# Float64 weights to float32: exponent and low bits made on ScalarE, two merging passes on VectorE

## Chip, cores and metric

The kernel runs on one core of a Trainium2 chip. The metric is the device time of one execution in microseconds; a run's time is that of its core. Engines are named as the profile names them: PE (TensorE matmul), PEld (its weight load), DVE (VectorE), ACT (ScalarE), SP (SyncE, which here issues every transfer).

## What is computed

Attention with 4 sink positions and a window of 128 over 2 batches, 8 heads, 768 positions and head size 64, then two two-layer blocks on the 1536 rows of width 512 that come out of it. The blocks' weights arrive as float64.

```python
x = attention(q, k, v)                  # 1536 x 512
h = x @ w_in                            # 512 x 2048
g = maximum(h, 0) + alpha * minimum(h, 0)
x = g @ w_out                           # 2048 x 512
h = x @ w_in2
out = (h - tanh(h)) @ w_out2
```

## The kernel before

The attention is done in 48 pairs of heads, numbered `n` (a unit of 128 positions has 4 pairs). A pair is scored on PE (`s_mm`), its maximum is taken on DVE (`s_max`), its exponential on ACT (`s_exp`), it is normalised on DVE (`norm`), turned on PE (`t_mm`), copied out of PSUM by ACT (`t_ev`), and multiplied with the values on PE (`pv`). Pairs 0 to 18 run alone (`for n in range(S_LEAD)`, line 526 on); pairs 19 to 47 run inside the blocks.

The blocks are 96 steps `g`: block `m` (0, 1), chunk `c` of 512 rows (3), slice `f` of 128 hidden units (16). Every product is made in three float32r matmuls out of a high and a low part of both factors. Step `g` makes `h` of its slice (`h_mm`, 12 matmuls, line 367) and the output share of the slice of two steps ago (`out_mm`, 12 matmuls, line 419); in steps 0 to 31 it also carries one pair of the attention. For block 0 the result of `h_mm` has one PSUM bank, which ACT empties (`evac_first`, line 374) before the next step's `h_mm` may write it.

Weights: slice `f` of a block is 2 x 512 KB of float64 (`load_w`). It lands in one of two staging halves (`raw`), is converted to float32 (`conv_w`, `convert_weights`, lines 47 to 60) into a `wf` tile that stays for the block's three chunks, and in every step a high part is made on ACT (`split_w`, line 195) and a low part on DVE (`split_lo`, line 200). Each `yield` in `convert_weights` is a place where the conversion may be split: `conv_start` issues the ACT pass, `conv_step` one DVE pass at a time.

```python
    nc.scalar.activation(out=dst, in_=hw.bitcast(F32), func=AF.Abs)          # line 52
    yield
    nc.vector.tensor_scalar(dst, dst, HW_LO, HW_HI, op0=ALU.max, op1=ALU.min)    # line 54
    yield
    nc.vector.tensor_scalar(di, di, 5, 2, ...)                                # line 56
    yield
    nc.vector.scalar_tensor_tensor(di, lw, 29, di, ...)                       # line 58
    yield
    nc.vector.scalar_tensor_tensor(di, hw, TOP2, di, ...)                     # line 60
```

The kernel is scheduled by hand: every engine runs its instructions in the order in which the code issues them. Block 0 is converted during the attention alone (slices 0 and 1, from pairs 8 and 12 on) and in steps 0 to 13 (one slice each); block 1 in steps 31 to 46 (three steps out of four) and three more slices by step 60. In a step of chunk 0 the DVE order is: norm of the pair before, the first conversion pass, `s_max`, `evac_mid`, two `split_lo`, `evac_lo`, the other conversion passes. At the end of the step ACT issues the first pass for the next slice (`conv_start(*ahead)`), and SP the load of the slice after that, which waits until its staging half has been read. In steps 33 and 39 `flag` and `flag_rest` test whether the inputs suit this fast path; the test's result guards a general path that is not taken here.

Of the kernel before, what the change touches and what calls it, by code (L numbers as in the profile page):

```python
# [12 lines left out]
U8 = mybir.dt.uint8  # L13
BF16 = mybir.dt.bfloat16
# [25 lines left out]
TOP2 = -0x40000000  # L40

# [6 lines left out]
def convert_weights(nc, pair, dst):  # L48

    lw, hw = pair[:, :, 0], pair[:, :, 1]  # L50
    di = dst.bitcast(I32)
    nc.scalar.activation(out=dst, in_=hw.bitcast(F32), func=AF.Abs)  # L52
    yield
    nc.vector.tensor_scalar(dst, dst, HW_LO, HW_HI, op0=ALU.max, op1=ALU.min)
    yield
    nc.vector.tensor_scalar(di, di, 5, 2, op0=ALU.logical_shift_left, op1=ALU.logical_shift_right)  # L56
    yield
    nc.vector.scalar_tensor_tensor(di, lw, 29, di, op0=ALU.logical_shift_right, op1=ALU.bitwise_or)  # L58
    yield
    nc.vector.scalar_tensor_tensor(di, hw, TOP2, di, op0=ALU.bitwise_and, op1=ALU.bitwise_or)  # L60

# [59 lines left out]
def fast_path(tc, qk, v, vsink, limits, w1i, w1o, alpha, w2i, w2o, out, outer):  # L121
# [3 lines left out]
    with ExitStack() as ctx:  # L125
# [15 lines left out]
        vs = const.tile([128, 4, 128], F32, name="vs")  # L141
        m_even = const.tile([128, 288], BF16, name="m_even")
# [38 lines left out]
        def conv_w(m, f):  # L181
            raw = stage[m][f % 2]
            if m == 1 and f < 3:
                wf[m, f] = ap.tile([128, 1024], F32, name="wf", tag="wx" if f == 2 else "pq", bufs=1 if f == 2 else 2)
            else:
                wf[m, f] = wp.tile([128, 1024], F32, name="wf", tag="wf", bufs=NF)
            yield from convert_weights(nc, raw.rearrange("p (n t) -> p n t", t=2), wf[m, f])
# [3 lines left out]
        def split_w(m, c, f, part):  # L191
# [3 lines left out]
            nc.scalar.activation(out=hi, in_=src, func=AF.Copy)  # L195
            whl[m, c, f, part] = (hi, lo)

        def split_lo(m, c, f, part):
            hi, lo = whl[m, c, f, part]
            nc.vector.tensor_tensor(lo, wf[m, f][:, 512 * part:512 * part + 512], hi, op=ALU.subtract)  # L200
# [156 lines left out]
        h_ps, gt, o_ps, mid, ob = {}, {}, {}, {}, {}  # L357

        def h_mm(m, c, f, lo, hi):
            x = (x_t, y_t)[m][c]  # L360
            if lo == 0:
                h_ps[f] = ps_tile(["h"] if m == 0 else ["h", "s", "t"])
# [223 lines left out]
        def flag():  # L586
# [8 lines left out]
            nc.vector.tensor_tensor(worst, worst, top, op=ALU.mult)  # L595
            flag_in.extend((ones, worst))
# [3 lines left out]
        def flag_rest():  # L600
            ones, worst = flag_in
            t = ps_tile(["t"])
# [19 lines left out]
        for g in range(N):  # L622
# [25 lines left out]
            if g == 2 * NF + 1:  # L648
                flag()
            if g == 2 * NF + 7:  # L650
# [306 lines left out]
```

## Time and profile before

| | us |
|---|---|
| three runs | 677.49, 677.59, 677.14 (median 677.49) |
| the profiled execution's span | 676.7 |
| its own time | not listed apart; the runs lie 0.4 to 0.9 over its span |
| PE busy in the span | 639.5 (95%) |
| DVE busy | 567.1 (84%) |
| ACT busy | 437.6 (65%) |

The span runs from the first to the last instruction of the program. The shares are means over stretches with different limits, so the stretches are read apart. A matmul of 512 columns is listed with some 0.39 us, though the next one starts 0.23 us after it: matmuls overlap, and the time of a stretch is read from the starts.

### The profile page before, as it was taken

The numbers are of one execution on the slowest core, as the hardware profiler recorded it, in microseconds if no ns is written. First come the engines' busy times: TensorE is split into PE (matmuls) and PEld (weight loads), VectorE is DVE, ScalarE is ACT, GpSimd is POOL, SyncE is SP. The second block draws the span as 40 slices with busy tenths as digits, with TensorE's granted clock in tenths as the row PEclk, the third lists the DMA queues.
The fourth block names the chain that finished last, engine by engine and source line by source line (L and its number), as shares of the span: only waits on it lengthen the run. The fifth ranks groups of instructions, "written<-read, shape, count | busy, mean of one in ns | idle before, by whom it ended". The sixth has DMA issues, their size and how long they took to land.

```text
span 676.7 us, 9202 instructions
## 1 busy us (share of the span) xinstructions
PE 639.5 (95%) x3194; PEld 502.8 (74%) x3194; DVE 567.1 (84%) x1159; ACT 437.6 (65%) x872; POOL 1.1 (0%) x8
## 2 busy tenths in 40 slices
PE   4878999999999999999899999999999999999995
PEld 2556667767777777777687888888888888888884
DVE  5898999999967566648999998999988878888873
ACT  4776766666656565544545557778777777777763
POOL 0000000000000000000000000000000000000000
PEclk9987999999999999999999999999999999999998
DMA  4653343445010000023333340100010000100001
GB/s 110 218 155 96 140 156 140 155 157 186 1 47 17 0 16 1 31 96 112 137 125 125 139 173 0 44 20 0 1 62 1 1 0 1 62 1 1 0 1 67
DMA packets 27031, 47.36 MB, mean 70 GB/s; under 512 B 3168, under 2 KB 15456, under 8 KB 26976
## 3 DMA queue, kind: packets, MB, share of 16 engines
q1 hardware_dynamic: 26976, 46.68, 20.2%
q8 instruction: 27, 0.44, 0.3%
q14 instruction: 28, 0.23, 0.1%
HBM read 43.53 MB, written 3.15 MB: 69 GB/s over the span
## 4 chain that ended last, share of the span: by engine, by line
PE 71%; DVE 18%; DMA 3%; ACT 3%; issue 2%; SPq 2%; ACTq 0%; DVEq 0%
PE ps_o L419 31%; PE ps_h L367 19%; PE ps_s L367 6%; PE ps_t L367 6%; DVE wf L58 3%; DVE wf L60 2%; DMA vt<-in_v_dram 2%; DVE wf L56 2%; DVE gl L403 2%; DVE pq L259 1%; DVE wl L200 1%; PE ps_s L250 1%; PE ps_t L299 1%; DVE pq L283 1%; PE ps_v L338 1%
## 5 line engine op out<-in xcount | busy, mean ns | idle before, releaser
L200 DVE TENSOR_TENSOR wl<-wf,wh 128x512 fp32r<-128x512 f32 x192 | 123.4, 682 | 44.1 <-ACT wh L195 44.1
L367 PE MATMUL ps_h<-x,wh 128*128 128x512 f32 x384 | 124.6, 405 | 4.6 <-ACT t L374 4.1
L195 ACT ACTIVATE wh<-wf 128x512 fp32r<-128x512 f32 x192 | 111.6, 629 | 26.4 <-DVE wf L60 10.1
L367 PEld LDWEIGHTS ps_h<-x,wh 128*128 128x128 f32 x384 | 68.3, 188 | 22.4 <-ACT t L374 7.6
L419 PE MATMUL ps_o<-gh,wh 128*128 128x512 f32 x192 | 76.6, 399 | 1.4 <-DVE y L430 1.4
L367 PE MATMUL ps_h<-x,wl 128*128 128x512 f32 x192 | 75.2, 392 | 0.0
L419 PE MATMUL ps_o<-wh,gh 128*128 128x512 f32 x192 | 74.8, 390 | 0.2 <-ACT gh L398 0.2
L419 PE MATMUL ps_o<-gh,wl 128*128 128x512 f32 x192 | 74.9, 390 | 0.0
L419 PE MATMUL ps_o<-gl,wh 128*128 128x512 f32 x192 | 74.8, 390 | 0.0
L419 PE MATMUL ps_o<-wh,gl 128*128 128x512 f32 x192 | 74.8, 390 | 0.0
L419 PE MATMUL ps_o<-wl,gh 128*128 128x512 f32 x192 | 74.7, 389 | 0.0
L268 ACT ACTIVATE pq<-pq,nm 128x288 f32<-128x288 f32 (+1 forms) x96 | 48.4, 507 | 32.1 <-DVE nm L259 32.1
L398 ACT ACTIVATE gh<-g 128x512 fp32r<-128x512 f32 x48 | 30.4, 633 | 37.7 <-DVE g L109 37.7
L398 ACT ACTIVATE gh<-t 128x512 fp32r<-128x512 f32 x48 | 30.1, 627 | 32.4 <-DVE t L386 32.4
L52 ACT ACTIVATE wf<-raw 128x1024 f32<-128x1024 f32 x32 | 36.7, 1147 | 16.7 <-DMA raw<-in_moe_w_out_dram 16.7
L419 PEld LDWEIGHTS ps_o<-gh,wh 128*128 128x128 f32 x192 | 36.0, 188 | 10.2 <-DVE y L430 1.8
L367 PEld LDWEIGHTS ps_h<-x,wl 128*128 128x128 f32 x192 | 36.0, 188 | 8.2
L419 PEld LDWEIGHTS ps_o<-wh,gh 128*128 128x128 f32 x192 | 36.0, 188 | 8.1 <-ACT gh L398 0.6
L419 PEld LDWEIGHTS ps_o<-wh,gl 128*128 128x128 f32 x192 | 36.0, 188 | 7.9 <-DVE gl L403 0.4
L419 PEld LDWEIGHTS ps_o<-gh,wl 128*128 128x128 f32 x192 | 36.0, 188 | 7.8
L419 PEld LDWEIGHTS ps_o<-wl,gh 128*128 128x128 f32 x192 | 36.1, 188 | 7.4
L419 PEld LDWEIGHTS ps_o<-gl,wh 128*128 128x128 f32 x192 | 36.1, 188 | 7.0
(142 smaller groups left out, 1274.5 us busy)
## 6 DMA issues: line engine op xcount, KB each, us to landing
raw<-in_moe_w_in_dram SPq DMA_DIRECT2D x32, 512.0 KB, 3.3
raw<-in_moe_w_out_dram SPq DMA_DIRECT2D x32, 512.0 KB, 4.3
raw_qk<-in_qk_dram SPq DMA_DIRECT2D x96, 64.0 KB, 3.0
vt<-in_v_dram SPq DMA_DIRECT2D x12, 256.0 KB, 3.1
out_dram<-ob SPq DMA_DIRECT2D x2, 1024.0 KB, 4.3
out_dram<-ob SPq DMA_DIRECT2D x4, 256.0 KB, 3.6
vs<-in_vsink_dram SPq DMA_DIRECT2D x2, 256.0 KB, 3.1
ns_raw<-in_limits_dram SPq DMA_DIRECT2D x1, 2.0 KB, 2.5
```

The source lines that it names most:

```text
L52: nc.scalar.activation(out=dst, in_=hw.bitcast(F32), func=AF.Abs)
L56: nc.vector.tensor_scalar(di, di, 5, 2, op0=ALU.logical_shift_left, op1=ALU.logical_shift_right)
L58: nc.vector.scalar_tensor_tensor(di, lw, 29, di, op0=ALU.logical_shift_right, op1=ALU.bitwise_or)
L60: nc.vector.scalar_tensor_tensor(di, hw, TOP2, di, op0=ALU.bitwise_and, op1=ALU.bitwise_or)
L195: nc.scalar.activation(out=hi, in_=src, func=AF.Copy)
L200: nc.vector.tensor_tensor(lo, wf[m, f][:, 512 * part:512 * part + 512], hi, op=ALU.subtract)
L250: nc.tensor.matmul(sps[n, a][:, :w], lhsT=kq[l][h, p, at:at + 128], rhs=kq[r][h, p, K_EVEN:K_EVEN + w], start=e == 0, stop=e == 2)
L268: nc.scalar.activation(out=e, in_=e, func=AF.Exp, scale=-1.0, bias=nm[:, 2 * n + a:2 * n + a + 1], accum_out=sums[G][:, hh:hh + 1])
L367: nc.tensor.matmul(h_ps[f], lhsT=l[:, w], rhs=x[:, r, kk, :], start=kk == 0 and e == 0, stop=kk == 3 and e == 2)
L398: nc.scalar.activation(out=gh, in_=mid[f], func=AF.Copy)
L403: nc.vector.tensor_tensor(gl, mid.pop(f), gt[f][0], op=ALU.subtract)
L419: nc.tensor.matmul(o, lhsT=l, rhs=r, start=f == 0 and e == 0, stop=f == NF - 1 and e == 2)
```

## The change

For the fast path, `convert_weights` (one ACT pass, four DVE passes) gives way to `convert_scaled` (two ACT passes, two DVE passes). ACT's first pass multiplies the high word, read as a float32, by 2 to the power of -111, which moves the exponent instead of masking it, and sums each row into `seen`; its second pass turns the upper 16 bits of the low word into the number of its top three bits and writes that back over the low word. DVE shifts the first result by 3 and joins the three bits, then joins the sign. The weights are now 256 times too large; `split_w` and `split_lo` take that out by a factor of 1/256, for which `split_lo` becomes a scalar_tensor_tensor. Three small DVE instructions test `seen`, and `flag` and `flag_rest` move from steps 33 and 39 to steps 65 and 71. `flag_rest` uses the PSUM bank `v`, and block 1 takes the banks `h`, `s`, `t` strictly in turn, where before the turn was also advanced by the four output banks of each chunk.

```diff
--- before.py
+++ after.py
@@ -11,6 +11,7 @@
 F32R = mybir.dt.float32r
 I32 = mybir.dt.int32
 U8 = mybir.dt.uint8
+U16 = mybir.dt.uint16
 BF16 = mybir.dt.bfloat16
 AF = mybir.ActivationFunctionType
 ALU = mybir.AluOpType
@@ -38,6 +39,10 @@
 HW_LO = 3.0517578125e-05
 HW_HI = 122879.9921875
 TOP2 = -0x40000000
+SIGN = -0x80000000
+W_UP, W_DOWN = 2.0 ** -111, 2.0 ** -8
+W_LIMIT = 61440.0 * W_UP
+FLOOR = -4095.5 / 8192
 
 P0, P1, P2 = 0.33333329098008546, -0.13331417165962514, 0.052681329087423304
 POLY_T2 = 0.04
@@ -60,6 +65,19 @@
     nc.vector.scalar_tensor_tensor(di, hw, TOP2, di, op0=ALU.bitwise_and, op1=ALU.bitwise_or)
 
 
+def convert_scaled(nc, pair, dst, seen):
+
+    lw, hw = pair[:, :, 0], pair[:, :, 1]
+    top = pair.bitcast(U16)[:, :, 1]
+    di = dst.bitcast(I32)
+    nc.scalar.activation(out=dst, in_=hw.bitcast(F32), func=AF.Abs, scale=W_UP, accum_out=seen)
+    nc.scalar.activation(out=lw, in_=top, func=AF.Copy, scale=1.0 / 8192, bias=FLOOR)
+    yield
+    nc.vector.scalar_tensor_tensor(di, di, 3, lw, op0=ALU.logical_shift_left, op1=ALU.bitwise_or)
+    yield
+    nc.vector.scalar_tensor_tensor(di, hw, SIGN, di, op0=ALU.bitwise_and, op1=ALU.bitwise_or)
+
+
 def load_scalars(nc, pool, limits):
 
     raw = pool.tile([128, 2, 2], I32, name="ns_raw")
@@ -139,6 +157,7 @@
         al = const.tile([128, NF], F32, name="al")
         nm = const.tile([128, 2 * NPAIR], F32, name="nm")
         vs = const.tile([128, 4, 128], F32, name="vs")
+        seen = const.tile([128, 2 * NF], F32, name="seen")
         m_even = const.tile([128, 288], BF16, name="m_even")
         m_odd = const.tile([128, 288], BF16, name="m_odd")
         m_one = const.tile([128, 288], BF16, name="m_one")
@@ -184,7 +203,8 @@
                 wf[m, f] = ap.tile([128, 1024], F32, name="wf", tag="wx" if f == 2 else "pq", bufs=1 if f == 2 else 2)
             else:
                 wf[m, f] = wp.tile([128, 1024], F32, name="wf", tag="wf", bufs=NF)
-            yield from convert_weights(nc, raw.rearrange("p (n t) -> p n t", t=2), wf[m, f])
+            at = m * NF + f
+            yield from convert_scaled(nc, raw.rearrange("p (n t) -> p n t", t=2), wf[m, f], seen[:, at:at + 1])
 
         whl = {}
 
@@ -192,12 +212,12 @@
             src = wf[m, f][:, 512 * part:512 * part + 512]
             hi = wp.tile([128, 512], F32R, name=f"wh{part}", tag=f"wh{part}", bufs=2)
             lo = wp.tile([128, 512], F32R, name=f"wl{part}", tag=f"wl{part}", bufs=2)
-            nc.scalar.activation(out=hi, in_=src, func=AF.Copy)
+            nc.scalar.activation(out=hi, in_=src, func=AF.Copy, scale=W_DOWN)
             whl[m, c, f, part] = (hi, lo)
 
         def split_lo(m, c, f, part):
             hi, lo = whl[m, c, f, part]
-            nc.vector.tensor_tensor(lo, wf[m, f][:, 512 * part:512 * part + 512], hi, op=ALU.subtract)
+            nc.vector.scalar_tensor_tensor(lo, wf[m, f][:, 512 * part:512 * part + 512], W_DOWN, hi, op0=ALU.mult, op1=ALU.subtract)
 
 
         x_t, y_t = {}, {}
@@ -355,11 +375,13 @@
 
 
         h_ps, gt, o_ps, mid, ob = {}, {}, {}, {}, {}
+        turn = [0]
 
         def h_mm(m, c, f, lo, hi):
             x = (x_t, y_t)[m][c]
             if lo == 0:
-                h_ps[f] = ps_tile(["h"] if m == 0 else ["h", "s", "t"])
+                turn[0] += m
+                h_ps[f] = ps_tile(["hst"[turn[0] % 3]])
             wh, wl = whl[m, c, f, 0]
             for kk in range(lo, hi):
                 w = slice(kk * 128, kk * 128 + 128)
@@ -593,13 +615,16 @@
             nc.vector.tensor_scalar(worst, worst, 9e8, None, op0=ALU.is_le)
             nc.vector.tensor_scalar(top, top, 1.0, None, op0=ALU.is_le)
             nc.vector.tensor_tensor(worst, worst, top, op=ALU.mult)
+            nc.vector.tensor_scalar(seen, seen, W_LIMIT, None, op0=ALU.is_lt)
+            nc.vector.tensor_reduce(top, seen, axis=AX.X, op=ALU.min)
+            nc.vector.tensor_tensor(worst, worst, top, op=ALU.mult)
             flag_in.extend((ones, worst))
 
         flag_in = []
 
         def flag_rest():
             ones, worst = flag_in
-            t = ps_tile(["t"])
+            t = ps_tile(["v"])
             nc.tensor.matmul(t[:, 0:1], lhsT=ones, rhs=worst, start=True, stop=True)
             ok = const.tile([1, 2], F32, name="ok")
             lim = const.tile([1, 2], F32, name="lim")
@@ -645,9 +670,9 @@
                 ahead = (1, start.get(g + 1, slow.get(g + 1)))
             if conv1 is not None and conv1 + 2 < NF:
                 load = (1, conv1 + 2)
-            if g == 2 * NF + 1:
+            if g == 4 * NF + 1:
                 flag()
-            if g == 2 * NF + 7:
+            if g == 4 * NF + 7:
                 flag_rest()
 
             if att and n - 2 < NPAIR:
```

VectorE in step 2 of block 0, before (the order of steps 0 to 13 is alike). `sums` and `pq<-pq,sums` are `norm`, ISA is `s_max`, `wl` is `split_lo`, `gl` is `evac_lo`, and `wf` are the conversion passes:

```order
L283 TENSOR_SCALAR pq<-pq,sums 128x288 x2
L54 TENSOR_SCALAR wf<-wf 128x1024
L259 ISA pq,nm<-ps_s,m_odd 128x288
L259 ISA nm 128x1
L259 ISA pq,nm<-ps_t,m_odd 128x288
L259 ISA nm 128x1
L386 SCALAR_TENSOR_TENSOR t<-t,al 128x512
L200 TENSOR_TENSOR wl_934<-wf,wh_933 128x512
L200 TENSOR_TENSOR wl_931<-wf,wh_930 128x512
L403 TENSOR_TENSOR gl<-t,gh 128x512
L56 TENSOR_SCALAR wf<-wf 128x1024
L58 SCALAR_TENSOR_TENSOR wf<-raw_89,wf 128x1024
L60 SCALAR_TENSOR_TENSOR wf<-raw_89,wf 128x1024
```

The same place now:

```order
L303 TENSOR_SCALAR pq<-pq,sums 128x288 x2
L76 SCALAR_TENSOR_TENSOR wf<-wf,raw_90 128x1024
L279 ISA pq,nm<-ps_s,m_odd 128x288
L279 ISA nm 128x1
L279 ISA pq,nm<-ps_t,m_odd 128x288
L279 ISA nm 128x1
L408 SCALAR_TENSOR_TENSOR t<-t,al 128x512
L220 SCALAR_TENSOR_TENSOR wl_932<-wf,wh_931 128x512
L220 SCALAR_TENSOR_TENSOR wl_929<-wf,wh_928 128x512
L425 TENSOR_TENSOR gl<-t,gh 128x512
L78 SCALAR_TENSOR_TENSOR wf<-raw_90,wf 128x1024
```

Of the conversion, one pass stands ahead of `s_max` and one behind `gl`, in place of one and three; `wl` has become a scalar_tensor_tensor.

ScalarE in the same step, before, from `s_exp` (`pq,sums`) to the copy `t_ev` (`pt<-ps_t`) of the next step; `gh` is `evac_hi`, `t<-ps_h` is `evac_first`:

```order
L268 ACTIVATE pq,sums<-pq,nm 128x288 x2
L398 ACTIVATE gh<-t 128x512
L374 ACTIVATE t<-ps_h 128x512
L52 ACTIVATE wf<-raw_89 128x1024
L214 ACTIVATE kq<-raw_qk 128x2x256
L306 ACTIVATE pt<-ps_t 128x512
L195 ACTIVATE wh_1009<-wf 128x512
```

The same place now:

```order
L288 ACTIVATE pq,sums<-pq,nm 128x288 x2
L420 ACTIVATE gh<-t 128x512
L396 ACTIVATE t<-ps_h 128x512
L73 ACTIVATE wf,seen<-raw_90 128x1024
L74 ACTIVATE raw_90<-raw_90 128x1024
L234 ACTIVATE kq<-raw_qk 128x2x256
L326 ACTIVATE pt<-ps_t 128x512
L215 ACTIVATE wh_1006<-wf 128x512
```

The second conversion pass (`raw<-raw`) stands between `evac_first` and what follows it: the next step's `t_ev`, and in every second step a `kq` copy ahead of that.

## Rows read from the trace of the kernel before

**Rows 1.** Stretches between step starts: length, busy PE, PEld, DVE, ACT, POOL; clock, DMA.

```profile
0.00:74.29 74.29, 54.03 (x369) 37.34 (x369) 61.72 (x234) 49.51 (x137) 1.14 (x8) 0.93 0.48 148
74.29:173.66 99.37, 94.12 (x494) 68.79 (x495) 97.64 (x208) 62.58 (x132) 0.00 (x0) 1.00 0.43 147
173.66:189.37 15.71, 15.55 (x88) 11.33 (x86) 12.77 (x31) 8.75 (x21) 0.00 (x0) 1.00 0.00 0
189.37:288.68 99.31, 99.07 (x577) 77.11 (x577) 65.80 (x177) 58.42 (x136) 0.00 (x0) 1.00 0.08 24
302.42:329.69 27.27, 23.79 (x109) 18.47 (x107) 24.10 (x39) 14.22 (x24) 0.00 (x0) 1.00 0.32 116
329.69:363.78 34.09, 33.51 (x147) 27.21 (x147) 32.73 (x53) 19.18 (x30) 0.00 (x0) 1.00 0.34 124
363.78:676.70 312.92, 305.66 (x1345) 251.84 (x1343) 266.09 (x410) 217.72 (x381) 0.00 (x0) 0.99 0.10 35
```

**Rows 2.** Chain that ended last: start us, us, what; two of its pieces.

```profile
346.48 2.72 PE ps_h L367 x12
...
418.34 2.97 PE ps_s L367 x12
```

**Rows 3.** DVE groups by line and shape: busy us, mean ns, idle before.

```profile
L200 DVE TENSOR_TENSOR wl<-wf,wh 128x512 fp32r<-128x512 f32 x192 | 123.4, 682 | 44.1 <-ACT wh L195 44.1
L58 DVE SCALAR_TENSOR_TENSOR wf<-raw,wf 128x1024 int32<-128x1024 int32 x32 | 39.2, 1224 | 0.9
...
L108 DVE SCALAR_TENSOR_TENSOR g<-b,g 128x512 f32<-128x512 f32 x48 | 32.7, 681 | 0.0
...
L54 DVE TENSOR_SCALAR wf<-wf 128x1024 f32<-128x1024 f32 x32 | 22.0, 687 | 1.6 <-ACT wf L52 1.6
```

**Rows 4.** ACT groups by line and shape.

```profile
L52 ACT ACTIVATE wf<-raw 128x1024 f32<-128x1024 f32 x32 | 36.7, 1147 | 16.7 <-DMA raw<-in_moe_w_out_dram 16.7
...
L268 ACT ACTIVATION_READ_ACCUMULATOR pq<-pq,nm 128x1 f32 x96 | 18.1, 189 | 0.0
```

**Rows 5.** DVE in order of time, step 12 and start of step 13 (start us, us).

```profile
161.42 0.17 DVE L274 TENSOR_SCALAR sums<-sums 128x2 f32<-128x2 f32 x1
...
162.38 0.69 DVE L54 TENSOR_SCALAR wf<-wf 128x1024 f32<-128x1024 f32 x1
162.99 0.45 DVE L259 CUSTOM_DVE_ANT_0 pq<-ps_s,m_one 128x288 f32<-128x288 f32 x1
...
169.33 0.16 DVE L274 TENSOR_SCALAR sums<-sums 128x2 f32<-128x2 f32 x1
```

**Rows 6.** ACT in order of time, from step 12 to the `t_ev` of step 13.

```profile
163.48 0.54 ACT L268 ACTIVATE pq<-pq,nm 128x288 f32<-128x288 f32 x1 [1.93 <-DVE nm L259]
...
165.53 1.15 ACT L52 ACTIVATE wf<-raw 128x1024 f32<-128x1024 f32 x1
166.57 0.63 ACT L214 ACTIVATE kq<-raw_qk 128x512 fp32r<-128x512 f32 x1
167.09 0.59 ACT L306 ACTIVATE pt<-ps_t 128x512 f32<-128x512 f32 x1
```

**Rows 7.** PE in step 13: the last score matmul of its pair.

```profile
168.11 0.29 PE L250 MATMUL ps_t<-kq 64*128 64x288 f32 x1
```

**Rows 8.** PE in order of time, 318 to 331 us: the three matmul groups that waited.

```profile
321.11 0.72 PE L367 MATMUL ps_h<-x,wh 128*128 128x512 f32 x2 [0.93 <-ACT t L374]
...
325.49 0.50 PE L419 MATMUL ps_o<-gh,wh 128*128 128x512 f32 x1 [1.35 <-DVE y L430]
...
329.69 0.74 PE L367 MATMUL ps_h<-x,wh 128*128 128x512 f32 x2 [1.21 <-ACT t L374]
```

**Rows 9.** ACT in order of time, the same stretch.

```profile
323.76 2.02 ACT L429 ACTIVATE y<-ps_o 128x512 fp32r<-128x512 f32 x4
```

**Rows 10.** DVE in order of time, the same stretch.

```profile
324.76 2.47 DVE L430 TENSOR_TENSOR y<-ps_o,y 128x512 fp32r<-128x512 f32 x4
...
327.75 0.74 DVE L386 SCALAR_TENSOR_TENSOR t<-t,al 128x512 f32<-128x512 f32 x1
```

## Prediction

> **What bounds the kernel now.** I read the chain that ended last first, then the busy times by stretch, then the groups and the order of time on each engine, to see what a conversion costs and who stands behind it.
>
> The edges of rows 1 are the first matmuls of steps 2, 14, 16, 29, then 31, 35 and 41. In the last half the chain is PE alone: pieces of twelve matmuls of 2.72 us, back to back, two to a step, so 5.44 us a step [rows 2]. No engine that only feeds PE can shorten that. The one blemish is a piece of 2.97, in step 51. The busy times show the same for steps 16 to 28: 99.31 us for 13 steps, 7.64 each with the attention inside, PE busy for 99.07, DVE for 65.80 [rows 1]. These stretches stay as they are.
>
> Steps 2 to 13 are another matter. They take 99.37 us, 8.28 each, and DVE is busy for 97.64 of them, 98% [rows 1]. They are the steps that convert one slice each. Steps 14 and 15, with the same order of code and no conversion, take 15.71 together, 7.86 each. So DVE bounds these twelve steps, by 0.4 us a step over the same code without conversion and by 0.64 over steps 16 to 28. The second such place is steps 31 to 40, where block 1 is converted: DVE is busy for 32.73 of the 34.09 of steps 35 to 40, and just before that three groups on PE waited [rows 1, 8]. What comes ahead of step 2 takes 74.29 us, DVE busy for 61.72, ACT for 49.51: neither engine alone; four slices are converted there.
>
> **The change part by part.** *DVE passes.* A slice loses L54 and L56, two of one form, 2 x 0.687 = 1.37 us [rows 3]. The two merges that remain read one strided and one dense operand, as L58 does, and I give them its 1.224. `split_lo` (L200) turns from 0.682 [rows 3] into a scalar_tensor_tensor with constants; that form on the same size takes 0.681 (L108), so nothing.
>
> *ACT passes.* The first pass stays (1.147 [rows 4]) and gains a row sum; the sum's read-out is the accumulator row, 0.189. The second pass is new. Its read is strided like that of L52, of which 1024 elements take 1.147; its write goes to every second word, and no row shows ACT writing so. From below 1.04, what L52 holds ACT up to the next start, 165.53 to 166.57 [rows 6]; from above 2.3, twice L52, if the strided write cost as much again as the read. I take 1.15, since strided reads and dense writes of the same count are the nearest row. The Trainium skill, page "SBUF — State Buffer", section "Door 1: The DMA port swizzle", says that accesses that fall at least twice into one 16-byte line go at full rate; words 8 bytes apart do, so by it the second pass would cost an estimated 1.15 and the sum below would stand, while a write that missed that rate would make it about 674. No row tells the two apart.
>
> So a slice gives DVE 1.37 back and gives ACT 0.19 + 1.15 = 1.34. What matters is who stands behind ACT. Behind the second pass wait, on ACT, the `kq` copy and `t_ev` of the next step; behind `t_ev` waits PE's next `s_mm` (its bank is the one that `t_ev` empties), behind that `s_max` on DVE, behind that `s_exp`, again on ACT. That ring closes once a step. Its present length: `s_exp` starts at 163.48, `t_ev` at 167.09 and ends at 167.68 [rows 6], the last score matmul ends at 168.40 [rows 7], and `s_max` to `s_exp` takes 0.49 (162.99 [rows 5] to 163.48), so the next `s_exp` could start at 168.89: 5.41 us, against the 7.91 that DVE needs from one `norm` to the next (161.42 to 169.33 [rows 5]). With 1.34 more the ring is 6.75, and 7.3 in the one step of four that has an `x` copy there. It stays under PE's 7.64. The first merge on DVE also waits for the second pass, but `norm` stands ahead of it and covers it: 0.96 from 161.42 to 162.38.
>
> *Steps 2 to 13.* DVE's need falls from 97.64 by 12 x 1.37 to 81.2, 6.8 a step. PE is then the longest. The gain is at least nothing and at most what PE's own work leaves: six of the twelve steps have the short first units of the second batch in them, with about 0.5 less attention than the 7.64 of steps 16 to 28, so 7.4 on average and 12 x (8.28 - 7.4) = 10.5. I choose 7.78 a step, just under the 7.86 of the steps without conversion, since rings this close to each other (6.8, 6.75 to 7.3, 7.4) don't run without loss: 12 x 0.5 = 6.0. Steps 14 and 15 start without a backlog on DVE: 0.3.
>
> *Ahead of step 2.* Four slices at 1.37 are 5.5 on DVE and 5.4 more on ACT. In the attention alone neither engine is full, and an ACT pass is on the way of `t_ev` and `s_exp` at once, while the DVE passes that go were spread over several pairs. From -2 to 4; I take 1.5, most of it in steps 0 and 1, which have the DVE order of the steps above.
>
> *Steps 31 to 40.* The three waits of PE end at 321.11, 325.49 and 329.69 and are 0.93 + 1.35 + 1.21 = 3.5 [rows 8]; steps 35 to 40 lose another 34.09 - 6 x 5.44 = 1.45 in small ones [rows 1]. All of it is DVE's backlog. I follow what replaces it. The conversion ahead of the copies of `y` holds ACT some 2.35 us instead of 1.1, but is reached 2.2 earlier, since the two merges before it end earlier; so the four copies, now at 323.76 [rows 9], start at about 322.9. DVE's part of them, 324.76 to 327.2 [rows 10], then ends at about 325.9, the first merge (1.24, where L54 took 0.6) at 327.2, and `evac_mid` starts there instead of at 327.75. So of the first three waits only 0.55 is won; the later ones, 1.45, go, as a step then needs 5.1 on DVE. Together 2.0, between 0 and 4.95. Step 51 loses its late bank: 2.97 - 2.72 = 0.25 [rows 2].
>
> *The flag.* Some ten small DVE instructions go from step 33 to step 65 and three come along. DVE is busy for 266.09 of the last 312.92 [rows 1], so they are covered; uncovered they would cost some 0.17 each, like the small DVE row at 161.42 [rows 5], 2.2 us.
>
> Sum: 6.0 + 0.3 + 1.5 + 2.0 + 0.25 = 10.05. The profiled span is 676.7; the median of the runs lies 0.8 over it, at 677.5. 676.7 - 10.0 + 0.8 = 667.5 us.
>
> **The rivals.** *The second pass is dear, and ACT's ring takes over (slower).* The ring without it is 5.41 + 0.19 = 5.6; it passes the present 8.28 once the pass costs over 2.7 us, 2.3 times L52. At 3.4 (three accesses for one) it is 9.0: 12 x 0.7 = 8.6 lost, some 4 ahead of step 2, so 690. For it speaks only that no row shows such a write; against it that the strided read costs hardly more than a dense one. Chance 0.06.
>
> *An exchange without profit.* 1.37 of DVE is paid with 1.34 of ACT; if ACT's passes hold up the pairs as much as DVE's did, or the pass costs 2.3 (ring 7.9, 8.4 with `x`), the time stays between 675 and 679. Against it: ACT is busy for 62.58 of 99.37 in steps 2 to 13 [rows 1]. Beside it stands the Trainium skill, page "ScalarE: Activation LUTs", section "Rules for kernel authors", which wants `max`, `min`, `add` and `mul` on VectorE and not on ScalarE. By that rule the time would stay at about 677; the rows agree on the price of one pass (0.687 against 1.147), not on which engine has room. Chance 0.08.
>
> *The staging halves hold ACT.* A load waits for the merge, ACT for the load (16.7 us in all [rows 4]), and a shorter step leaves the load less time. If half the gain of the twelve steps and of steps 31 to 40 goes, the sum is 6 and the time 671.5. Chance 0.17.
>
> *PE at once the only limit.* All of 10.5, 0.3, 4, 4.95 and 0.25: 657.5; more likely something over it, about 660. Chance 0.11.
>
> My own case keeps 0.58. The range takes it with its unknowns (3 a side) and the staging rival, 662 to 674.
>
> A measurement of this kernel tells 0.2%, 1.4 us, from no change. Faster by more: 0.58 + 0.17 + 0.11 and a fifth of the exchange, 0.88; slower: 0.06 and a little of the exchange, 0.07; the same: 0.05.
>
> **What would show it.** In the new profile: steps 2 to 13 at 7.6 to 7.9 us, DVE busy there for some 87% and no longer without gaps; the new ACT pass at 1.05 to 1.25; `t_ev` waiting for nothing that delays `s_mm` by over half a microsecond; steps 16 to 28 at 7.64 and the last half at 5.44 as before; the third wait of rows 8 still there, the small ones after it gone. Wrong would be a second pass of over 2 us, DVE waiting for it ahead of its first merge, or steps 2 to 13 at over 8.1.

## The result, and the profile after

The changed kernel takes 672.85 us (median of 4 runs, 671.23 to 673.67) against 677.54 of the kernel before beside it: ratio 0.992, with a 95% interval from 0.9902 to 0.9939. So it is 4.7 us faster, where 10.0 were forecast. The profiled execution has a span of 670.3, and its run took 672.06.

The stretches of the changed kernel, between the same step starts as in [rows 1] except that step 0 has an edge of its own (62.38). The columns are the length, then busy PE, PEld, DVE, ACT and POOL with counts, then the granted clock, the DMA share and GB/s:

```profile
0.00:62.38 62.38, 42.22 (x304) 29.15 (x304) 49.09 (x203) 41.90 (x120) 1.14 (x8) 0.95 0.51 157
62.38:76.14 13.76, 12.02 (x66) 8.49 (x67) 10.36 (x25) 12.47 (x28) 0.00 (x0) 0.88 0.28 96
76.14:168.11 91.97, 90.42 (x497) 67.49 (x496) 83.70 (x188) 74.18 (x156) 0.00 (x0) 1.00 0.45 158
168.11:183.43 15.32, 15.28 (x88) 11.31 (x86) 8.42 (x24) 8.76 (x21) 0.00 (x0) 1.00 0.00 0
183.43:282.69 99.26, 99.03 (x577) 77.10 (x577) 65.83 (x177) 58.43 (x136) 0.00 (x0) 1.00 0.08 24
296.42:322.28 25.86, 23.81 (x109) 18.47 (x107) 20.00 (x27) 17.35 (x30) 0.00 (x0) 1.00 0.33 122
322.28:355.06 32.78, 32.78 (x145) 27.14 (x146) 26.00 (x35) 24.08 (x39) 0.00 (x0) 1.00 0.35 129
355.06:670.30 315.24, 307.17 (x1347) 251.37 (x1345) 256.65 (x410) 226.42 (x397) 0.00 (x0) 1.00 0.09 34
```

Beside [rows 1] these say where the time went. Steps 2 to 13 went from 99.37 to 91.97, and PE is now busy for 98% of them and DVE for 91%: the heart of the forecast. Steps 31 to 40 gave 1.4 and 1.3. But everything ahead of step 2 grew from 74.29 to 76.14, with a granted clock of 0.88 in steps 0 and 1, and from step 41 on the kernel lost 2.3 us (312.92 to 315.24). The span fell by 6.4, more than the medians did (4.7): the profiled execution of the kernel before was one of its slower ones, that of the changed kernel one of its faster ones (reckoned below).

In the last half the chain is PE as before, 5.44 us from one step to the next (start us, length, what; answers to [rows 2]):

```profile
641.14 2.72 PE ps_s L389 x12
646.58 2.72 PE ps_t L389 x12
```

Of the three waits of [rows 8] the first is gone, and of 3.49 us 2.05 are left (PE in order of time):

```profile
317.55 0.50 PE L441 MATMUL ps_o<-gh,wh 128*128 128x512 f32 x1 [0.34 <-DVE y L452]
...
322.28 0.73 PE L389 MATMUL ps_h<-x,wh 128*128 128x512 f32 x2 [1.71 <-ACT t L396]
```

The groups of the conversion by line (busy us, mean ns of one, then idle time before it with its releaser). L220 is `split_lo`, L76 and L78 are the two merges, L73 and L74 the two ACT passes:

```profile
L220 DVE SCALAR_TENSOR_TENSOR wl<-wf,wh 128x512 fp32r<-128x512 f32 x192 | 123.6, 685 | 45.2 <-ACT wh L215 45.2
...
L76 DVE SCALAR_TENSOR_TENSOR wf<-wf,raw 128x1024 int32<-128x1024 int32 x32 | 39.1, 1222 | 18.7 <-ACT raw L74 18.6
L78 DVE SCALAR_TENSOR_TENSOR wf<-raw,wf 128x1024 int32<-128x1024 int32 x32 | 39.0, 1220 | 0.0
L73 ACT ACTIVATE wf<-raw 128x1024 f32<-128x1024 f32 x32 | 36.5, 1142 | 6.6 <-DMA raw<-in_moe_w_out_dram 6.6
...
L74 ACT ACTIVATE raw<-raw 128x1024 int32<-128x1024 uint16 x32 | 36.2, 1132 | 0.0
```

Every price is as forecast: the new pass 1.132 where I took 1.15, the merges 1.22, the split 0.685. The staging wait of the first pass went from 16.7 [rows 4] to 6.6. New is the 18.6 in which the first merge waited for the second pass, 13 times.

**Step 0.** ACT in order of time (start us, us):

```profile
62.83 1.12 ACT L73 ACTIVATE wf<-raw 128x1024 f32<-128x1024 f32 x1
...
63.94 1.09 ACT L74 ACTIVATE raw<-raw 128x1024 int32<-128x1024 uint16 x1
64.93 0.59 ACT L326 ACTIVATE pt<-ps_t 128x512 f32<-128x512 f32 x1
65.40 0.28 ACT L345 ACTIVATE pts<-ps_s 128x128 f32<-128x128 f32 x1
```

And PE in the same place, whose score matmuls (L270) need the banks that `t_ev` (L326) and the sink copy (L345) empty:

```profile
63.61 0.39 PE L389 MATMUL ps_h<-x,wl 128*128 128x512 f32 x1
65.74 0.40 PE L270 MATMUL ps_s<-kq 64*128 64x288 f32 x1 [1.74 <-ACT pts L345]
```

Both ACT passes stand ahead of the two copies that PE waits for. The same row in the kernel before:

```profile
64.47 0.40 PE L250 MATMUL ps_s<-kq 64*128 64x288 f32 x1 [0.72 <-ACT pts L325]
```

The wait was 0.72; it is 1.74 now. Step 0 took 5.55 us there and 7.89 here, counted from one step's first `h_mm` to the next one's.

**Step 51.** ACT (first fence) and DVE (second) in order of time, in steps 48 to 51:

```profile
400.99 1.13 ACT L73 ACTIVATE wf<-raw 128x1024 f32<-128x1024 f32 x1
...
402.12 1.11 ACT L74 ACTIVATE raw<-raw 128x1024 int32<-128x1024 uint16 x1
...
405.31 2.05 ACT L451 ACTIVATE y<-ps_o 128x512 fp32r<-128x512 f32 x4
```

```profile
401.51 0.69 DVE L425 TENSOR_TENSOR gl<-g,gh 128x512 fp32r<-128x512 f32 x1
405.93 2.48 DVE L452 TENSOR_TENSOR y<-ps_o,y 128x512 fp32r<-128x512 f32 x4 [3.74 <-ACT y L451]
```

The waits of that stretch (in all, times, longest) close the chain:

```profile
DVE y L452 <- ACT y L451: 3.7, 1, 3.7
...
PE ps_s L389 <- DVE wl L220: 1.0, 1, 1.0
```

The pair of ACT passes of a late slice delays the copies of `y`, DVE idles 3.74 for them, `split_lo` behind it comes late, and PE waits 1.0. Step 51 went from 5.69 to 6.77.

### The profile page after: what moved, and what is told of

It is laid out like the page before. It is cut to its first block, busy times and chain, and to the rows that moved or that the text cites. A ratio compares the mean times of both kernels' runs of the same rounds, so it can differ in the third digit from the quotient of the medians.

```text
span 670.3 us, 9201 instructions
## 1 busy us (share of the span) xinstructions
PE 636.5 (95%) x3194; PEld 501.2 (75%) x3194; DVE 526.3 (79%) x1098; ACT 471.9 (70%) x936; POOL 1.1 (0%) x8
## 4 chain that ended last, share of the span: by engine, by line
PE 80%; DVE 8%; ACT 7%; issue 2%; SPq 1%; DMA 1%; ACTq 0%; DVEq 0%
PE ps_o L441 34%; PE ps_h L389 22%; PE ps_s L389 7%; PE ps_t L389 6%; PE ps_t L319 2%; PE ps_s L270 2%; PE ps_v L358 2%; PE ps_v L359 2%; PE ps_v L362 2%; ACT raw L74 1%; ACT wf L73 1%; PE ps_o L270 1%; DVE wf L78 1%; SPq L180 1%; DVE pq L279 1%
## 5 line engine op out<-in xcount | busy, mean ns | idle before, releaser
L220 DVE SCALAR_TENSOR_TENSOR wl<-wf,wh 128x512 fp32r<-128x512 f32 x192 | 123.6, 685 | 45.2 <-ACT wh L215 45.2
L76 DVE SCALAR_TENSOR_TENSOR wf<-wf,raw 128x1024 int32<-128x1024 int32 x32 | 39.1, 1222 | 18.7 <-ACT raw L74 18.6
L326 ACT ACTIVATE pt<-ps_t 128x512 f32<-128x512 f32 (+1 forms) x39 | 21.8, 560 | 35.5 <-PE ps_t L319 35.5
```

Of the source, the lines that this page charges most:

```text
L76: nc.vector.scalar_tensor_tensor(di, di, 3, lw, op0=ALU.logical_shift_left, op1=ALU.bitwise_or)
L220: nc.vector.scalar_tensor_tensor(lo, wf[m, f][:, 512 * part:512 * part + 512], W_DOWN, hi, op0=ALU.mult, op1=ALU.subtract)
L326: nc.scalar.activation(out=ptb[n][:, :, e0:, :], in_=tv[:, :, e0:, :], func=AF.Copy)
```

## Experiments

All were timed in five rounds beside the kernel before, whose median was 677.85 to 677.97 there and 677.54 beside the change; differences of a few tenths between these kernels say nothing. The question was what the second ACT pass really costs, and how much of that belongs to its place in ACT's order.

### No second pass

```diff
-    nc.scalar.activation(out=lw, in_=top, func=AF.Copy, scale=1.0 / 8192, bias=FLOOR)
...
-    nc.vector.scalar_tensor_tensor(di, di, 3, lw, op0=ALU.logical_shift_left, op1=ALU.bitwise_or)
+    nc.vector.scalar_tensor_tensor(di.rearrange('p (a b) -> p a b', b=128), di.rearrange('p (a b) -> p a b', b=128), 3, none.unsqueeze(1).to_broadcast([128, 8, 128]), op0=ALU.logical_shift_left, op1=ALU.bitwise_or)
```

`none` is a tile of zeros that is set once at the start (not shown).

> The changed kernel without ScalarE's second pass; the first merge on VectorE joins zeros instead, so the low three bits of the weights are left out. Theory: the second pass stands ahead of t_ev on ScalarE, which costs PE 1.7 us and a lower clock in step 0 and 1.0 us in step 51; without it step 0 falls from 7.9 to about 5 us, step 51 from 6.8 to 5.5, steps 2 to 13 from 91.97 to 89 to 91; span about 665, time some 5 us under the changed kernel. Rival: step 0 and step 51 are long for another reason (the merge's place ahead of s_max, the turn of the PSUM banks); then both stay and the time falls by under 2 us.

Measured: 662.91 us (661.70 to 665.21), ratio 0.9777 (0.9764 to 0.979). The merge that joins zeros takes as long as the other (1.221 for 1.222), so the difference is the pass. That is 9.9 under the changed kernel, twice what I had set for it. Its profiled run was the slowest of the five, so its stages, in the table further on, rather understate the gain: steps 0 and 1 are 2.4 shorter than in the changed kernel, steps 2 to 13 1.7, 31 to 34 1.5, 48 to 61 1.7. The second pass costs something in every stage with a conversion, not only in step 0.

### A third pass of the first kind

```diff
     nc.scalar.activation(out=lw, in_=top, func=AF.Copy, scale=1.0 / 8192, bias=FLOOR)
+    nc.scalar.activation(out=dst, in_=hw.bitcast(F32), func=AF.Abs, scale=W_UP)
```

> The changed kernel with one more ScalarE pass per slice (the first pass made again, without its row sum), nothing left out. Theory: another 1.05 us on ScalarE ahead of t_ev; step 0 grows by 1 to 2, step 51 by about 1, and steps 2 to 13 from 91.97 by 2 to 10, since the ring of 6.75 goes to 7.8 and passes PE's 7.4; time 5 to 14 us over the changed kernel. Rival: ScalarE has slack everywhere; under 2 us.

Measured: 696.97 (694.0 to 697.54), ratio 1.0276 (1.0258 to 1.0293): 24 us over the changed kernel for another 1.1 us of ACT per slice, far above the range expected. Waits of this kernel (its L77 is the first merge):

```profile
DVE wf L77 <- ACT wf L75: 31.8, 20, 4.0
...
PE ps_t L271 <- ACT pt L327: 5.8, 4, 1.9
```

The merge now waits 31.8 us, and PE directly for ACT. The first added pass cost 9.9, the next one 24. By stage (table further on), 7.2 of that lie in steps 2 to 13, which went from 7.66 to 8.27 each. I read this part as the ring through ACT, which was just at PE's length with one added pass and is over it with two; that is argued and not shown. The ring can't explain the rest: 5.0 lie in the pairs ahead of step 0 and 7.4 in steps 41 to 61, where the attention is over. The granted clock was lower too, 0.977 over the span against 0.991; how much of the 24 that is was not tried.

### The second pass behind `t_ev`, both merges behind `evac_lo`

One added `yield` moves instructions, since `conv_start` and `conv_step` each issue up to the next one. In steps 0 to 13 and 31 to 46 the second pass is then issued where the first merge was, so on ACT it stands behind `t_ev`, the sink copy and the splits, ahead of `s_exp`, and both merges stand behind `evac_lo`; in the pairs ahead of step 0 the three pieces come one pair later.

```diff
     nc.scalar.activation(out=dst, in_=hw.bitcast(F32), func=AF.Abs, scale=W_UP, accum_out=seen)
+    yield
     nc.scalar.activation(out=lw, in_=top, func=AF.Copy, scale=1.0 / 8192, bias=FLOOR)
```

> The changed kernel with one more yield between ScalarE's two passes, so that the second is issued one conversion step later: in a step of block 0 behind t_ev and the two high splits and ahead of s_exp, where ScalarE waits for VectorE, with both merges behind evac_lo; during the pairs one pair later. The work is the same, nothing left out. Theory (the second pass costs because of its place ahead of t_ev, and VectorE's first merge because it waits for it ahead of s_max): most of the 10 us by which the kernel without that pass is faster comes back, steps 0 and 1 take about 11.5 instead of 13.77, steps 2 to 13 90 to 91 instead of 91.97, step 34 under 7.2; time 664 to 668. Rival (the pass costs by its length, wherever it stands): 671 to 674.

Measured: 666.74 (666.05 to 666.95), ratio 0.9832 (0.9819 to 0.9844): 6.1 under the changed kernel, with the same instructions. ACT in its step 0:

```profile
62.99 1.12 ACT L73 ACTIVATE wf<-raw 128x1024 f32<-128x1024 f32 x1
...
64.10 0.59 ACT L327 ACTIVATE pt<-ps_t 128x512 f32<-128x512 f32 x1
64.58 0.28 ACT L346 ACTIVATE pts<-ps_s 128x128 f32<-128x128 f32 x1
...
65.25 1.13 ACT L75 ACTIVATE raw<-raw 128x1024 int32<-128x1024 uint16 x1
66.28 0.53 ACT L289 ACTIVATE pq<-pq,nm 128x288 f32<-128x288 f32 x1
```

Its PE row in the same place, and its first merge in the groups by line:

```profile
64.91 0.40 PE L271 MATMUL ps_s<-kq 64*128 64x288 f32 x1 [0.76 <-ACT pts L346]
```

```profile
L77 DVE SCALAR_TENSOR_TENSOR wf<-wf,raw 128x1024 int32<-128x1024 int32 x32 | 39.0, 1219 | 0.3 <-ACT raw L75 0.3
```

The pass lies where ACT waited for `s_max` anyway, PE's wait is back at 0.76, and of the 18.6 us in front of the merge 0.3 are left. Of the 9.9 us that the second pass cost, 6.1 belonged to its place and that of the merges, and not to its work.

### The merges alone later

The first merge of a step goes out with the second, in the `conv_step(*conv, 3)` that stands behind `evac_lo` already.

```diff
-                if conv:
-                    conv_step(*conv)
                 h_mm(m, c, f, 0, 2)
```

> The changed kernel with ScalarE's two passes together where they are, but in the steps of block 0 the first merge behind evac_lo, next to the second. It tells the two halves of what the extra yield did apart. If the merge's wait for the second pass ahead of s_max was the cost: most of the 6 us come back, 666 to 669. If the pass's place ahead of t_ev was: PE's wait ahead of s_mm in step 0 stays and the time is 670 to 673. I hold the second likelier for steps 0 and 1, the first for steps 5, 9 and 13: about 670.

Measured: 671.29 (670.11 to 671.95), ratio 0.9906 (0.9891 to 0.9922), not told apart from the changed kernel. PE in step 0, and the stretch in which the changed kernel has its steps 0 and 1 (here they lie from 62.31 to 75.61, 13.30 us), for its granted clock:

```profile
65.67 0.40 PE L270 MATMUL ps_s<-kq 64*128 64x288 f32 x1 [1.72 <-ACT pts L345]
```

```profile
62.38:76.14 13.76, 11.04 (x68) 7.86 (x68) 9.63 (x25) 12.82 (x29) 0.00 (x0) 1.00 0.27 96
```

The wait in step 0 stays, as both passes are still ahead of the copies; steps 31 to 34 gain 1.2, since nothing waits ahead of `evac_mid`; steps 2 to 13 gain nothing.

### The second pass alone later

```diff
+    yield
     nc.scalar.activation(out=lw, in_=top, func=AF.Copy, scale=1.0 / 8192, bias=FLOOR)
...
-                    conv_step(*conv)
+                    conv_step(*conv, 2)
```

> The kernel with the extra yield, but the first merge taken up at once behind the second pass, ahead of s_max as in the changed kernel. If only the pass's place ahead of t_ev had cost, the time is near 667; if the merge that waits ahead of s_max costs as well, s_max now waits for a pass that starts later still, and the time is 668 to 674.

Measured: 681.68 (681.18 to 684.44), ratio 1.0055 (1.0042 to 1.0069), slower than the kernel before and over the 668 to 674 of the second reading. Its first merge by line, and the place of it in a step (DVE in order of time):

```profile
L77 DVE SCALAR_TENSOR_TENSOR wf<-wf,raw 128x1024 int32<-128x1024 int32 x32 | 39.2, 1224 | 42.8 <-ACT raw L75 42.8
```

```profile
150.25 0.65 DVE L304 TENSOR_SCALAR pq<-pq,sums 128x288 f32<-128x288 f32 x2
152.36 1.22 DVE L77 SCALAR_TENSOR_TENSOR wf<-wf,raw 128x1024 int32<-128x1024 int32 x1 [1.47 <-ACT raw L75]
153.50 0.45 DVE L280 CUSTOM_DVE_ANT_0 pq<-ps_s,m_one 128x288 f32<-128x288 f32 x1
```

DVE stands still for 1.47 us behind `norm` (L304), and `s_max` (L280) is behind the merge. The four orders, in us (in the lower row the added `yield` also moves the pieces in the pairs and in the late slices, by one pair or one step):

| | merges early | merges late |
|---|---|---|
| second pass early | 672.85 (the change) | 671.29 |
| second pass late | 681.68 | 666.74 |

Here the pass moved later is a gain only if its consumer moves too, and the two moves together give more than their sum.

### Three that moved one suspected cost

The conversion of step 0 a little later:

```diff
-        conv_start(0, len(CONV0))
...
+                if g == 0:
+                    conv_start(0, len(CONV0))
...
-                if conv:
+                if conv and g:
```

> The changed kernel, but in step 0 both ScalarE passes are issued behind t_ev and the high split, and both merges behind evac_lo; nothing left out. Theory: PE's wait of 1.74 us in step 0 goes, and with it the fall of the granted clock behind it; steps 0 and 1 take 10.5 to 11.5 instead of 13.77, time 2 to 3 us under the changed kernel. Rival: the wait only moves behind (ScalarE's passes delay s_exp or evac_first as much); within 0.7 us of the changed kernel.

Measured: 672.30 (670.62 to 673.83), ratio 0.9924 (0.991 to 0.9938). In the profiled run steps 0 and 1 took 12.40 where 10.5 to 11.5 were expected, 1.4 less than in the changed kernel: step 0 fell to 5.43, but step 1 rose from 5.88 to 6.97, so part of the wait only moved. The median is 0.55 lower, which can't be told from nothing.

The late slices two steps later, away from the copies of `y`:

```diff
-        slow = {CONV1 + 18 + 4 * k: len(start) + k for k in range(NF - len(start))}
+        slow = {CONV1 + 20 + 4 * k: len(start) + k for k in range(NF - len(start))}
```

> The changed kernel, but the last three slices of block 1 are converted two steps later (from steps 51, 55, 59), away from the copies of y at step 49; nothing left out. Theory: ScalarE's two passes stand ahead of y's copies and of the tanh of step 49, which makes the high split and its low part late for step 51; PE's wait of 1.03 there goes and so do the small ones of 0.1 in steps 52 to 61; time 1.5 to 2 us under the changed kernel. Rival: the wait is from the turn of the banks and stays; 0 to 0.3 us.

Measured: 672.47 (672.14 to 674.04), ratio 0.9928 (0.9915 to 0.9941). Step 51 is back at 5.72 in the trace, 1.05 less, and steps 48 to 61 take 77.2 for 78.4: the cause of that loss is confirmed in the trace. The median moved by 0.4 only, where 1.5 to 2 were expected, and that can't be told from nothing.

The first split three pairs later:

```diff
-                if n == at + 6 and f == 0:
+                if n == at + 9 and f == 0:
```

> The changed kernel with the first split of step 0 at pair 17 instead of pair 14 alone; nothing left out. Theory: as above, step 0 begins 1 to 3 us earlier than at 62.4, time 670 to 672. Rival: no difference.

Measured: 671.90 (670.36 to 674.71), ratio 0.9925 (0.991 to 0.9939). It is not told apart from the changed kernel. The pairs ahead of step 0 differ by 1 to 2 us between the traces (61.4 to 63.6 in those with two passes or fewer, and 62.4 and 63.6 for the same code of the pairs), which covers effects of this size. The trace shows something else: step 0 took 5.57 and steps 0 and 1 12.29, with the order of the changed kernel on ACT. ACT began its first pass at 60.65, 1.3 us ahead of the step's start at 61.95 (PE had waited 3.46 for `norm` just before); the copies were done early, and PE's wait of 1.74 is not there.

### Banks and flag without the conversion

```diff
-                h_ps[f] = ps_tile(["h"] if m == 0 else ["h", "s", "t"])
+                turn[0] += m
+                h_ps[f] = ps_tile(["hst"[turn[0] % 3]])
...
-            t = ps_tile(["t"])
+            t = ps_tile(["v"])
...
-            if g == 2 * NF + 1:
+            if g == 4 * NF + 1:
...
-            if g == 2 * NF + 7:
+            if g == 4 * NF + 7:
```

> The kernel before the change with the banks h, s, t strictly in turn and the two parts of the flag in steps 65 and 71, and nothing else of the change. Theory: step 33 loses 0.65 us of VectorE work in a backlog, step 51 its late bank of 0.25, and steps 70 and 71 gain 0.1 to 0.3: 0.3 to 1.0 us under the kernel before. Rival: the turn makes another bank late and step 51 longer, as it is in the changed kernel (6.77); then 0.5 to 1 us over.

Measured: 676.66 (675.41 to 677.36), ratio 0.9981 (0.9973 to 0.999), 1.3 under the 677.93 beside it, a little more than expected. Step 39 fell from 6.31 to 5.44; step 51 stayed at 5.71. The kernel before shows why, in DVE's order of time there:

```profile
354.89 0.14 DVE L606 TENSOR_SCALAR ok<-ps_t 1x1 f32<-1x1 f32 x1
...
356.20 0.14 DVE L614 CAST bad_i<-ok 1x1 int32<-1x1 f32 x1
356.27 0.73 DVE L386 SCALAR_TENSOR_TENSOR t<-t,al 128x512 f32<-128x512 f32 x1
...
359.21 0.69 DVE L54 TENSOR_SCALAR wf<-wf 128x1024 f32<-128x1024 f32 x1 [0.41 <-ACT wf L52]
359.82 0.74 DVE L386 SCALAR_TENSOR_TENSOR t<-t,al 128x512 f32<-128x512 f32 x1
```

Nine instructions on one element each (L606 to L614) held `evac_mid` (L386) back by 1.38 us in a step where it was already the last to come. Steps 31 to 34 took 26.9 here for 27.3, steps 35 to 40 32.9 for 34.1, and steps 70 and 71 0.3 more than before. So, if the parts add up, some 1.3 of the 4.7 us by which the changed kernel is faster come with the flag and not with the conversion. The bank in turn was no cure for step 51.

### Versions that go further

The added `yield` with the first split three pairs later:

```diff
+    yield
     nc.scalar.activation(out=lw, in_=top, func=AF.Copy, scale=1.0 / 8192, bias=FLOOR)
...
-                if n == at + 6 and f == 0:
+                if n == at + 9 and f == 0:
```

> The kernel before this one, and the first high and low split of step 0 made at pair 17 instead of pair 14. Theory: at pair 14 VectorE waits for ScalarE's high split, with s_max behind it, and PE waits 4.1 us, after which its granted clock falls to the lower level; with the split later the wait is under 2 us and the pairs end 1 to 3 us earlier; time 1 to 3 us under the kernel before this one. Rival: another wait takes its place at pair 17; within 0.7 us.

Measured: 666.16 (665.36 to 666.77), ratio 0.9826 (0.9813 to 0.9838). It is the lowest of the kernels that compute everything, 11.8 under the kernel before it ran beside (677.93), and its interval lies clear of the changed kernel's. It is not told apart from the `yield` alone. On top of it, the late slices moved by two steps (first below) and by one:

```diff
-        slow = {CONV1 + 18 + 4 * k: len(start) + k for k in range(NF - len(start))}
+        slow = {CONV1 + 20 + 4 * k: len(start) + k for k in range(NF - len(start))}
```

> The extra yield, the first split at pair 17, and the last three slices two steps later. Expected as the sum of its parts: steps 48 to 61 from 77.4 to about 76.9, time 665 to 666.2, the fastest of the kernels that leave nothing out. Rival: the waits of steps 51 to 61 only move; 666 to 667.

Measured: 665.09 (663.68 to 665.91), ratio 0.9806 (0.979 to 0.9823). This kernel leaves out the signs of some weights: for the first chunk of block 1, the half of the last slice that `h_mm` uses is split before its second merge. Every instruction is there, only one order is another. Steps 48 to 61 take 76.4, what they took in the kernel before, against 77.4 with the `yield` alone.

```diff
-        slow = {CONV1 + 18 + 4 * k: len(start) + k for k in range(NF - len(start))}
+        slow = {CONV1 + 19 + 4 * k: len(start) + k for k in range(NF - len(start))}
```

> The extra yield, the first split at pair 17, and the last three slices one step later instead of two, so that the last of them is merged before it is split; nothing left out. ScalarE's first pass for slice 13 then stands behind the copies of y in step 49 instead of ahead of them. Theory: step 51 falls from 5.8 to 5.5 and the time is 665 to 666, the fastest that computes all. Rival: as the kernel with the extra yield and the late split, 666.2.

Measured: 667.11 (666.24 to 669.41), ratio 0.9852 (0.9829 to 0.9874): step 51 at 5.69, but steps 48 to 61 still 77.3, so one step is no gain.

The stages from the traces, each from the first `h_mm` of its first step, in us (one profiled run each):

| kernel | pairs | 0–1 | 2–13 | 31–34 | 35–40 | 41–47 | 48–61 |
|---|---|---|---|---|---|---|---|
| before | 62.1 | 12.2 | 99.4 | 27.3 | 34.1 | 38.1 | 76.4 |
| the change | 62.4 | 13.8 | 92.0 | 25.9 | 32.8 | 38.6 | 78.4 |
| no second pass | 63.3 | 11.4 | 90.3 | 24.4 | 32.8 | 38.1 | 76.7 |
| third pass | 67.4 | 15.9 | 99.2 | 28.0 | 33.7 | 43.0 | 81.5 |
| pass and merges late | 62.5 | 11.6 | 91.5 | 24.1 | 32.8 | 38.1 | 77.4 |
| merges alone late | 62.3 | 13.3 | 92.0 | 24.7 | 32.8 | 38.4 | 78.4 |
| pass alone late | 62.6 | 15.2 | 94.5 | 27.6 | 34.3 | 44.2 | 77.3 |

Steps 14 to 30 took 128.8 in the kernel before and 128.3 in all of these, and steps 62 on 198.1 to 198.8.

## Why the prediction was right, and where it was not

The direction and its main cause came out as forecast; the size was twice too large, 10.0 for 4.7. The sum was 10.05 off the span, and the span fell by 6.4; that is 3.65 of the miss. The other 1.7 lies in the executions that were profiled. I set the runs 0.8 over their spans, but every run that is listed with its span, of either kernel, lies 1.7 to 1.9 over it (672.06 for 670.3). So the profiled execution of the kernel before, with its 676.7, must have taken an estimated 678.5, 1.0 over its median, and that of the changed kernel ran 0.8 under its own.

That the time lies inside the stated range is in part luck. My own case with 3 us a side ends at 670.5; the range reached to 674 for the staging rival, which did not act (below). And of the signs of being wrong that I had named, one came: DVE waits for the second pass ahead of its first merge, 18.6 us in all.

**The price of the second pass: right.** 1.132 against 1.15. That the strided write costs no more than a dense one is what the estimate by the Trainium skill, page "SBUF — State Buffer", section "Door 1: The DMA port swizzle", had given; the trace agrees (1.132 against 1.142 for the first pass, which writes densely).

**What the two engines exchange: smaller on both sides than I counted.** DVE's busy time in steps 2 to 13 fell by 13.94, 1.16 a slice and not 1.37: a pass that is listed with 0.69 lets the next instruction start after 0.61 (the two last rows of the fence on the kernel before, above). In the same way the second ACT pass holds ACT for 0.99 (63.94 to 64.93). In these steps that costs at most the 1.7 by which the kernel without the pass is shorter there (90.3 for 92.0), since PE is busy for 98% of them.

**Steps 2 to 13: right, and a little low.** 7.4 gained where 6.0 were put, 7.66 a step where I had 7.78. The sentence that `norm` covers the merge's wait for the second pass holds here: the twelve merges waited 0.1 us in all. Steps 14 and 15 gave 0.39 for 0.3.

**Ahead of step 2: the failed step.** "I take 1.5, most of it in steps 0 and 1, which have the DVE order of the steps above." The DVE order is the same, but not the hour at which ACT starts. In step 0 the first pass starts only 0.45 after the step, behind the `s_exp` of the pair before, so both passes end after `norm` does, `t_ev` is late, and the merge waits 1.0 in each of these two steps. In the profiled run the stretch lost 1.85 instead of winning 1.5, so 3.35 on the wrong side, though just inside the -2 to 4 that I had given it. The rows of ACT that I had read for the ring [rows 6] were of step 12; step 0 had the same code and another phase: in steps 1 to 13 of the changed kernel the first pass starts 0.7 to 3.2 ahead of its step. Where it started 1.3 ahead of step 0 too, in the kernel with the first split at pair 17, steps 0 and 1 took 12.29, about as before (12.18). Of the 1.85, steps 0 and 1 make 1.58. About 1.1 of this is the wait: with the same ACT order in step 0 and a clock of 1.00, the kernels with the merges alone later and with the late slices moved took 13.30 and 13.27. The other 0.5 is the fall of the granted clock in this one run (below), and the 0.27 left, in the pairs, is less than they differ between traces.

**Steps 31 to 40: a fair sum from wrong parts.** 2.7 for 2.0. The first four steps gave 1.41, not 0.55, and the third wait of [rows 8] stays, as forecast, and grew from 1.21 to 1.71. But much of the 2.7 is the flag, which I had put at nothing: by the kernel with banks and flag alone it is 0.4 of the 1.41 and 1.15 of the 1.31, 0.87 of it in step 39. Nine of its instructions stand there, and not in step 33 as I had it. I had called them covered because DVE was busy for 266 of 313 us: an average over a half, for instructions that stand in one step. The other slip is `norm`: from step 32 on the attention's part of DVE is over and nothing stands ahead of the merge. DVE in order of time in two such steps of the changed kernel:

```profile
349.89 1.23 DVE L76 SCALAR_TENSOR_TENSOR wf<-wf,raw 128x1024 int32<-128x1024 int32 x1 [2.76 <-ACT raw L74]
...
363.20 1.23 DVE L76 SCALAR_TENSOR_TENSOR wf<-wf,raw 128x1024 int32<-128x1024 int32 x1 [2.99 <-ACT raw L74]
```

Ten of the thirteen waits lie from here on, in steps 33 to 46, 15.9 of the 18.6 us. In steps 31 to 34 they cost 1.2, by the kernel with the merges alone later (24.7 for 25.9); in steps 35 to 40 they cost nothing (32.8 in both).

**From step 41 on: the other failed step.** I had 0.25 won by the late bank of step 51. The bank does nothing there (5.71 with it in turn), and the second ACT pass, which I had not followed into the late slices at all, takes 1.08 in step 51, about 1 more in small waits of steps 52 to 61, and 0.5 in steps 42 and 43; without that pass steps 48 to 61 take 76.7 and steps 41 to 47 38.1, nearly as before. It was 2.3 lost where 0.25 was to be won, 2.6 on the wrong side. The two failed steps make 5.9, of which the better stretches, 2 to 15 and 31 to 40, gave 2.2 back: the 3.65.

**The rivals.** The time lies nearest to the staging rival's 671.5, but its mechanism didn't act: the first pass waits less for its load than before. A dear second pass is excluded by 1.132, an exchange without profit by steps 2 to 13. Of the latter, the Trainium skill's page "ScalarE: Activation LUTs", section "Rules for kernel authors", had spoken for leaving `max` and `min` on VectorE. Here too a pass is cheaper on VectorE (0.687 against 1.132); the time fell all the same, by 4.7 and with a better order by 11.8. PE as the limit (about 660) is nearly reached only by the kernel that leaves the second pass out, at 662.9.

Left open: about 3.8 us between the kernel with the `yield` and the one without the pass (with the `yield` the first pass waits 16.5 us for its loads again, where it waited 6.6 in the change; what that costs was not tried), and 24 us for a third pass, of which the split between the ring, the other stages and the lower clock was not measured.

## What to carry to other kernels

When work moves to an engine with a low busy share, read that engine's order in every stage in which the work occurs (the first step, the last slices, the steps without the usual neighbours), not in one step that is typical: here the typical twelve were right, and the first two steps and the late slices gave back 4.2 of the 10.5 us won elsewhere. Where a generator feeds in-order engines, end a piece behind each instruction, also between two of the same engine, so that an added pass can be put where its engine waits, and move its consumer with it. A small instruction is covered or not by what stands behind it in its own step; the busy share of a half tells nothing about that.

## What the runs showed of the hardware

After PE's wait of 1.74 in step 0 the granted clock fell for some 6 us. The changed kernel by stretch, columns as in the first fence:

```profile
62.38:65.74 3.36, 1.62 (x9) 1.03 (x9) 1.66 (x5) 3.36 (x9) 0.00 (x0) 1.00 0.00 0
65.74:68.50 2.76, 2.76 (x14) 1.71 (x15) 2.50 (x7) 1.61 (x5) 0.00 (x0) 0.78 0.02 6
68.50:72.00 3.50, 3.50 (x20) 2.67 (x19) 2.42 (x7) 3.46 (x6) 0.00 (x0) 0.69 0.50 167
```

0.78 and 0.69 lie between the two levels, so parts of these stretches ran at 1.2 GHz and the rest at 2.4. PE had been busy for 1.62 of the 3.36 us before. But the kernel with the merges alone later has the same wait, 1.72, and a clock of 1.00 throughout, and so has the one with the late slices moved, whose first steps are those of the changed kernel (1.73); their step 0 took 6.57 and 6.54 instead of 7.89. So the wait doesn't decide it alone, and what does was not found. The fall costs 1.3 us in step 0, of which step 1 gives back most: together the two steps took 13.76 against 13.30 and 13.27. A longer wait of PE stands in the pairs of the same trace:

```profile
52.43 1.08 PE L319 MATMUL ps_h<-ident,pq 128*128 128x128 f32 x4 [4.14 <-DVE pq L303]
```

Behind it the granted clock was 0.50, the lower level, from 52 to 56 us; the kernel before shows the same 0.50 there, behind a wait of 3.08.

An ACT pass that reads 16-bit words and writes every second 32-bit word took 1.132 us for 1024 elements a partition, no more than one that reads every second 32-bit word and writes densely (1.142). The row sum of the first pass adds an instruction of 0.195.
